# Attention units taken two at a time on TensorE, in a recurrence followed by a feed-forward layer

## The chip, the core and the metric

The kernel runs on one core of one Trainium2 chip. The metric is the device time of one execution in microseconds (us). A core has a matrix engine (TensorE, PE in the profile, with PEld for its weight loads), VectorE (DVE), ScalarE (ACT), GpSimd (POOL) and SyncE (SP), whose queue issues all DMAs of this kernel. Matrix products are written to PSUM, which has eight banks of 128 partitions by 512 fp32 columns.

## The reference, cut to what matters

```python
# 4 batches, 8 heads, 768 tokens, head_dim D=32, state N=16, chunk 32
log_a = np.log(np.clip(a, 1e-06, 1.0))
for c in range(S // 32):                       # chunks of 32 tokens
    cum = np.cumsum(la, axis=-1)               # la: log_a of this chunk
    L = np.exp(cum[:, :, :, None] - cum[:, :, None, :]) * causal
    M = np.einsum('bhin,bhjn->bhij', Cc, Bc) * L
    y_intra = np.einsum('bhij,bhjd->bhid', M, xc)
    y_inter = np.einsum('bhin,bhnd->bhid', Cc, state) * np.exp(cum)[..., None]
    y[:, :, sl] = y_intra + y_inter
    Bx = np.einsum('bhjn,bhjd->bhjnd', Bc, xc) * decay_from_j
    state = decay_full * state + np.sum(Bx, axis=2)
x = y as [3072 tokens, 256]
h = x @ w_in                                   # w_in 256 x 2048
g = np.maximum(h, 0) + np.log1p(np.exp(-np.abs(h)))
out = g @ w_out                                # w_out 2048 x 256
```

## The kernel before, in words

**Attention.** A unit is 128 tokens of one batch, all 8 heads; there are 24 units (4 batches of 6). For unit i, on TensorE: `score` makes two tiles sp (B by C products; for units 8 to 11 each is a 64-row product of 512 columns, L386; from unit 12 each is two full-array products of 256 columns, L391); `update` makes zp, the unit's contribution to the state (L416, four products on 32 of the array's columns, seen as 8 instructions); `read` multiplies the state before the unit with C into yp (L450, 32 rows by 64 columns of the array, 8 instructions; not for the first unit of a batch); `within` adds the products inside the unit to yp (L466, 32 columns of the array, 16 instructions). Around them VectorE and ScalarE make m from sp (`weigh`, L402), state and tb from zp, y from yp times the growth gg (`grow`, L477), and split y into a high and a low part xh, xl for the feed-forward layer (L480, L485). GpSimd makes the mask rm.

**Feed-forward.** Tokens go in six chunks of 512 (four units each). A step (j, k) is chunk j and 128 of the 2048 hidden columns: `first` makes hp with six products of 512 columns (L563); ScalarE applies softplus into e (L591) and copies it to gh (L597), VectorE makes gl = e - gh (L603); `second` adds six more products of 512 columns to two accumulators acc (L642). `second` of a step stands 8 steps behind its `first` (LAG). The buffers: e 3, gh 4, gl 4; six PSUM banks (`ps`) for hp, sp, zp, yp and others; two banks for acc.

**Order.** The first part, units 0 to 7 and 20 steps with the splitting of the weights, is a written list (ORDER), kept in that order on all engines; its instructions stand in the profile under L127, the line of the helper. From step 20 on nothing pins TensorE, VectorE, ScalarE or GpSimd: a scheduler with its own model of the times places each instruction, by order of the program where several are ready. DMAs on SP keep the order of the program everywhere. In the program, unit i has its place at step s = 20, 22, 25, 28 for units 8 to 11 and (i - 4)*4 after that: `prepare` and `attend_scores` at s, `attend_values` (spread, update, read, within, grow, rest) one or two steps later, and the loads of unit i + 2 at s + 1.

**Loads.** A unit's data is one tile un (3 buffers): x, B, C by token and by row (`U_S` columns) and, behind them, the rows for the scores. `split_unit` makes b_rows and c_rows from it for units from 12 on; c_rows has one buffer and is filled by two DMAs from c_all. The growth gg is loaded for three units at once.

Of the kernel before, what the change touches and what calls it, by code (L numbers as in the profile page):

```python
# [10 lines left out]
F32 = mybir.dt.float32  # L11
# [4 lines left out]
ALU = mybir.AluOpType  # L16
PSUM = bass.MemoryType.PSUM

P = 128
NB, NH, S, D, N = 4, 8, 768, 32, 16  # L20
# [51 lines left out]
LAG = 8  # L72
WRAW = 4
EARLY = 8
U_STEP = (20, 22, 25, 28)


def constants():
# [26 lines left out]
def recurrence_then_ffn(ctx: ExitStack, tc: tile.TileContext, fst, un, at, al, w_in, w_out, const, outT):  # L105
# [12 lines left out]
    class InOrder:  # L118
# [4 lines left out]

        def __getattr__(self, name):
            f = getattr(self.engine, name)
            if in_order[0]:
                return lambda *a, **k: tc.keep_in_program_order(f(*a, **k))  # L127
            return f

# [4 lines left out]
    def load(out, in_):  # L134

        tc.keep_in_program_order(nc.sync.dma_start(out, in_))  # L136
# [46 lines left out]
    def growth_on_chip(i, n):  # L183

        if i == 0:
            gg = p2.tile([P, 2, GU * P], F32, tag="gg", name="gg0")
            for v in range(GU):
                gg_s[v] = gg[:, :, v * P : v * P + P]
        gp = ps.tile([P, 512], F32, tag="ps", name=f"gp{i}")
        sums = kc[:, : NC * (P + SUB)].rearrange("p (c k) -> p c k", k=P + SUB)[:, :, :SUB]  # L190
        for v in range(n):
            for g in range(2):
                h0 = 2 * (i + v) + g
                PE.matmul(
                    gp[:, (2 * v + g) * P : (2 * v + g + 1) * P].rearrange("p (c k) -> p c k", k=SUB),
                    by_column[0][:, h0 * P : h0 * P + P],
                    sums,
                    start=True,
                    stop=True,
                )  # L200
        yield
        for v in range(n):
            A.activation(
                gg_s[i + v], gp[:, 2 * v * P : 2 * (v + 1) * P].rearrange("p (g t) -> p g t", g=2), AF.Exp, scale=-1.0
            )


    un_s, gg_s, st = {}, {}, {}

    def load_unit(i):  # L210
        if i < HEAD:
            un_s[i] = head_in["h"][:, i]
            load(un_s[i], fst[i, :, :U_S])
            return
        un_s[i] = p3.tile([P, U_END], F32, tag="un", name=f"un{i}")
        if i < FIRST:
            load(un_s[i][:, :F_END], fst[i])
        else:
            load(un_s[i], un[i - FIRST])


    def load_head_c(i):
# [1 line left out]

    def load_growth(i):
        b, u = divmod(i, NU)
        if u % GU == 0:
            gg = p2.tile([P, 2, GU * P], F32, tag="gg", name=f"gg{i}")
            for g in range(2):
                src = gd[b, g * 4 : g * 4 + 4, u * P : (u + GU) * P].unsqueeze(1).broadcast_to([4, D, GU * P])  # L230
                load(gg[:, g, :], src)
            for v in range(GU):
                gg_s[i + v] = gg[:, :, v * P : v * P + P]


    c_rows = cp.tile([P, NQ, 2, P], F32R, name="c_rows")

    def split_unit(i):
        if i < FIRST:
            return  # L240
        t = un_s[i]
        b_rows = p2.tile([P, NQ, P], F32R, tag="b_rows", name=f"b_rows{i}")

        def split(out, j):
            raw = t[:, U_S + j * NQ * P : U_S + (j + 1) * NQ * P].rearrange("p (q t) -> p q t", q=NQ)
            g, be = (kb[:, C_GB + v : C_GB + v + 1] for v in (2 * j, 2 * j + 1))
            A.activation(out, raw, AF.Copy, scale=be)
            V.scalar_tensor_tensor(out, raw, g, out.bitcast(F32), op0=ALU.mult, op1=ALU.add)

        c_all = p2.tile([P, NQ, P], F32R, tag="c_all", name=f"c_all{i}")  # L250
        split(c_all, 1)
        for e in range(2):
            rows = slice(64 * e, 64 * e + 64)
            load(c_rows[rows, :, e].bitcast(F32), c_all[rows].bitcast(F32))
        split(b_rows, 0)
        st[i] = b_rows
# [72 lines left out]
    def x_parts(t0):  # L329
        j = max(i for i in range(len(sizes)) if starts[i] <= t0)  # L330
        if j not in xparts:
            xparts[j] = [p3.tile([P, 2, 512], F32R, tag=f"x{v}", name=f"x{v}_{j}", bufs=3) for v in "hl"]
        return xparts[j], t0 - starts[j]
# [22 lines left out]
    def scale_b(i):  # L356
        b, u = divmod(i, NU)
        if u < NU - 1:
            bp = mid[i]["bp"] = p2.tile([P, NH, N], F32, tag="bp", name=f"bp{i}", bufs=3)
            V.tensor_tensor(  # L360
                bp,
                un_s[i][:, U_B:U_C].rearrange("p (h n) -> p h n", n=N),
                f_tok[b][0][:, u, :].unsqueeze(2).broadcast_to([P, NH, N]),
                op=ALU.mult,
            )
# [12 lines left out]
    def score(i, g):  # L378
        sp = mid[i]["sp", g] = ps.tile([P, 512], F32, tag="ps", name=f"sp{i}_{g}")
        if i < FIRST:  # L380
            rows = slice(64 * g, 64 * g + 64)
            if i < HEAD:
                t = head_in["l"][rows, i]
                PE.matmul(sp, t[:, :P], t[:, P:], start=True, stop=True)
                return
            PE.matmul(sp, un_s[i][rows, U_S : U_S + P], un_s[i][rows, U_S + P : F_END], start=True, stop=True)  # L386
            return
        b_rows = st[i]
        for v in range(2):
            q = 2 * g + v  # L390
            PE.matmul(  # L391
                sp[:, 2 * v * P : 2 * (v + 1) * P],
                b_rows[:, q],
                c_rows[:, q].rearrange("p e t -> p (e t)"),
                start=True,
                stop=True,
            )
# [11 lines left out]
    def update(i):  # L409

        b, u = divmod(i, NU)
        if u < NU - 1:
            bp = mid[i]["bp"]
            zp = ps.tile([P, 512], F32, tag="ps", name=f"zp{i}")
            for q in range(NQ):
                PE.matmul(  # L416
                    zp[32 * q : 32 * q + 32, : 2 * D],
                    bp[:, 2 * q : 2 * q + 2, :].rearrange("p h n -> p (h n)"),
                    un_s[i][:, U_X + 2 * q * D : U_X + 2 * (q + 1) * D],
                    start=True,  # L420
                    stop=True,
                )
            yield
            state[i] = p2.tile([P, 2 * D], F32, tag="state", name=f"state{i}", bufs=3)
            if u == 0:
                V.tensor_copy(state[i], zp[:, : 2 * D])
            else:
                V.scalar_tensor_tensor(
                    state[i], state[i - 1], f_row[b][:, u, NC : NC + 1], zp[:, : 2 * D], op0=ALU.mult, op1=ALU.add
                )  # L430

    def spread(i):

        if i % NU > 0:
            tb = mid[i]["tb"] = p2.tile([P, 2, D], F32, tag="tb", name=f"tb{i}", bufs=3)
            V.tensor_tensor(
                tb,
                state[i - 1].rearrange("p (e d) -> p e d", d=D),
                bd.unsqueeze(2).broadcast_to([P, 2, D]),
                op=ALU.mult,  # L440
            )
# [45 lines left out]
    def whole(steps):  # L487
        for _ in steps or ():
            pass

    def attend_scores(i):
        decays(i)
        for g in range(2):
            score(i, g)
            weigh(i, g)
        scale_b(i)
        scale_c(i)

    def attend_values(i):
        for f in (spread, update, read, within, grow, rest):  # L500
            whole(f(i))

# [168 lines left out]

    def prefetch(i):
        if i < NB * NU:
            load_unit(i)
            load_growth(i)

    def prepare(i):
        split_unit(i)  # L680
# [71 lines left out]
    def values(s):  # L752
        j, k = steps[s - LAG]
        if s - LAG >= DONE:
            second(j, k)
            if k == NFT - 1:
                finish(j)
            elif k == HALF - 1 and j < 2:
                keep_sums(j)
# [4 lines left out]
    def plan(s, f, *args):  # L764
        fills[s].append((f, args))

    for i in range(EARLY, NB * NU):
        s, wait = (U_STEP[i - EARLY], 1) if i - EARLY < len(U_STEP) else ((i - HEAD) * NFT // 4, 2)
        plan(s, prepare, i)
        plan(s, attend_scores, i)  # L770
        plan(s + wait, attend_values, i)
        if i + 2 < NB * NU:
            plan(s + 1, prefetch, i + 2)
    for i in range(EARLY, EARLY + 2):
        prefetch(i)
    for s in range(AHEAD, len(steps) + LAG):
        if s < len(steps):
            first(*steps[s])
            for _ in parts_of(*steps[s]):
                pass  # L780
        values(s)
        for f, args in fills[s]:
            f(*args)


# [48 lines left out]
```

## Time and profile before

| | |
|---|---|
| median of 3 runs | 341.94 us (340.47 to 342.95) |
| span of the profiled execution, first to last instruction | 338.8 us |
| PE busy | 328.7 us, 97% |
| DVE, ACT, POOL busy | 202.8, 171.7, 39.3 us |
| granted TensorE clock | 1.000 |

The page gives the span of the profiled execution, 338.8 us, and no other time for it; the runs' median is 3.1 us above the span. In the profile's rows, a group is named by its line, engine and operation, then what it writes and reads. In the timeline, the columns are the start in us, the us from the start of a piece to its end, and the piece; the ends of matrix products are modelled and neighbours overlap, so what a product costs is read from one start to the next.

### The profile page before, as it was taken

Reading aid. Unit: us, or ns where it says so; the run is one execution under the profiler, and the core shown is the slowest. Engines: PE = TensorE matmul, PEld = TensorE weight load, DVE = VectorE, ACT = ScalarE, POOL = GpSimd, SP = SyncE. Lnnn points to the kernel's source line nnn. Section 1 sums busy time; section 2 is a strip of 40 time slices with the busy share of each in tenths; the row PEclk is TensorE's granted clock in tenths of the full one; section 3 lists DMA queues with packets and bytes.
Section 4 is the critical chain, followed back from the end, with each engine's and each line's share of the span. In section 5 each row is a group of like instructions: output and inputs, shape, how many; then the busy total and the mean of one; then the engine's idle time right before and its main releaser. Section 6 shows DMA issues by size and latency. Waiting matters only on the chain.

```text
span 338.8 us, 5271 instructions
## 1 busy us (share of the span) xinstructions
PE 328.7 (97%) x2047; PEld 249.4 (74%) x2047; DVE 202.8 (60%) x394; ACT 171.7 (51%) x319; POOL 39.3 (12%) x32
## 2 busy tenths in 40 slices
PE   8789998999999999999999999999999999999995
PEld 4446657887666678778778778778778778888885
DVE  0899989996946444864765464777474342232242
ACT  4845666875715435445445455445445244444450
POOL 2434510000111010110112010111010000000000
PEclk9999999999999999999999999999999999999999
DMA  7964533573032205416434205443203100010001
GB/s 233 396 228 138 220 106 104 188 259 120 3 98 114 93 0 189 133 39 186 126 61 141 95 0 188 122 106 99 94 2 93 33 0 0 2 55 8 2 0 62
DMA packets 19376, 35.01 MB, mean 103 GB/s; under 512 B 1432, under 2 KB 10136, under 8 KB 19352
## 3 DMA queue, kind: packets, MB, share of 16 engines
q1 hardware_dynamic: 19352, 34.68, 31.5%
q8 instruction: 16, 0.26, 0.3%
q14 instruction: 8, 0.07, 0.1%
HBM read 28.28 MB, written 3.24 MB: 93 GB/s over the span
## 4 chain that ended last, share of the span: by engine, by line
PE 86%; DVE 6%; DMA 5%; SPq 1%; issue 1%; ACT 0%
PE hp L563 32%; PE acc L642 32%; PE hp L127 6%; PE acc L127 6%; PE yp L466 3%; DMA gg<-gd 3%; DMA head_in_l<-in_fst 2%; PE yp L450 2%; PE sp L391 2%; DVE m L127 1%; DVE w L127 1%; PE sp L386 1%; SPq L136 1%; PE zp L416 1%; PE end L127 1%
## 5 line engine op out<-in xcount | busy, mean ns | idle before, releaser
L603 DVE TENSOR_TENSOR gl<-e,gh 128x512 fp32r<-128x512 f32 x76 | 55.7, 734 | 61.3 <-ACT gh L597 61.1
L597 ACT CAST gh<-e 128x512 fp32r<-128x512 f32 x76 | 47.1, 620 | 61.1 <-PE acc L642 60.3
L591 ACT ACTIVATE e<-hp 128x512 f32<-128x512 f32 x76 | 45.1, 596 | 42.4 <-DVE gl L603 38.5
L563 PE MATMUL hp<-xh,wih 128*128 128x512 f32 x152 | 61.3, 405 | 0.0
L642 PE MATMUL acc<-gl,woh 128*128 128x512 f32 x155 | 60.6, 391 | 0.0
L642 PE MATMUL acc<-gh,wol 128*128 128x512 f32 x155 | 60.5, 391 | 0.0
L642 PE MATMUL acc<-gh,woh 128*128 128x512 f32 x155 | 59.6, 391 | 0.0
L563 PE MATMUL hp<-xl,wih 128*128 128x512 f32 x152 | 59.5, 392 | 0.0
L563 PE MATMUL hp<-xh,wil 128*128 128x512 f32 x152 | 59.3, 391 | 0.0
L345 POOL TENSOR_SCALAR_AFFINE_SELECT rm<-fc 128x1024 f32<-128x1024 f32 x16 | 23.8, 1487 | 187.7 <-DVE m L402 167.8
L563 PEld LDWEIGHTS hp<-xh,wih 128*128 128x128 f32 x152 | 28.5, 188 | 10.7 <-issue 3.1
L642 PEld LDWEIGHTS acc<-gh,woh 128*128 128x128 f32 x155 | 29.1, 188 | 6.8 <-issue 0.8
L642 PEld LDWEIGHTS acc<-gh,wol 128*128 128x128 f32 x155 | 29.1, 188 | 6.2
L642 PEld LDWEIGHTS acc<-gl,woh 128*128 128x128 f32 x155 | 29.1, 188 | 6.1 <-issue 0.2
L563 PEld LDWEIGHTS hp<-xh,wil 128*128 128x128 f32 x152 | 28.5, 188 | 6.3
L563 PEld LDWEIGHTS hp<-xl,wih 128*128 128x128 f32 x152 | 28.6, 188 | 5.1
L402 DVE TENSOR_TENSOR m<-sp,rm 128x512 f32<-128x512 f32 x32 | 20.9, 685 | 7.9 <-PE sp L391 6.3
L127 DVE SCALAR_TENSOR_TENSOR w<-wraw,w 128x512 int32<-128x512 int32 x32 | 23.1, 729 | 0.2
L127 PE MATMUL hp<-xh,wih 128*128 128x512 f32 (+1 forms) x48 | 17.7, 368 | 2.0 <-DVE m L127 1.4
L127 PE MATMUL hp<-xl,wih 128*128 128x512 f32 (+1 forms) x48 | 17.0, 354 | 0.0
L127 PE MATMUL hp<-xh,wil 128*128 128x512 f32 (+1 forms) x48 | 17.0, 354 | 0.0
L127 POOL TENSOR_SCALAR_AFFINE_SELECT rm<-fc 128x1024 f32<-128x1024 f32 x8 | 14.0, 1764 | 20.8 <-DVE m L127 15.0
(109 smaller groups left out, 409.6 us busy)
## 6 DMA issues: line engine op xcount, KB each, us to landing
un<-in_un SPq DMA_DIRECT2D x12, 768.0 KB, 4.4
un<-in_fst SPq DMA_DIRECT2D x8, 576.0 KB, 6.1
wraw<-in_w_in SPq DMA_DIRECT2D x8, 512.0 KB, 3.4
wraw<-in_w_out SPq DMA_DIRECT2D x8, 512.0 KB, 5.2
c_rows<-c_all SPq DMA_DIRECT2D x24, 128.0 KB, 2.4
out_t<-o SPq DMA_DIRECT2D x11, 256.0 KB
gg<-gd SPq DMA_DIRECT2D x14, 192.0 KB
head_in_l<-in_fst SPq DMA_DIRECT2D x4, 320.0 KB, 6.2
```

Of the source, the lines that this page charges most:

```text
L127: return lambda *a, **k: tc.keep_in_program_order(f(*a, **k))
L136: tc.keep_in_program_order(nc.sync.dma_start(out, in_))
L345: Pl.affine_select(out=rm.rearrange("p h c i -> p (h c) i"), in_=fc[:, u].rearrange("p h c -> p (h c)").unsqueeze(2).broadcast_to([P, NH * ...
L391: PE.matmul(sp[:, 2 * v * P : 2 * (v + 1) * P], b_rows[:, q], c_rows[:, q].rearrange("p e t -> p (e t)"), start=True, stop=True,)
L402: V.tensor_tensor(mid[i]["m"][:, 4 * g : 4 * g + 4].rearrange("p h t -> p (h t)"), mid[i].pop(("sp", g)), mid[i]["rm"][:, 4 * g : 4 * g + ...
L450: PE.matmul(yp[q // 2][out], tb[rows].rearrange("p e d -> p (e d)"), cc[rows].rearrange("p c i -> p (c i)"), start=True, stop=False,)
L466: PE.matmul(yp[g][32 * hh : 32 * hh + 32], un_s[i][:, U_X + h * D : U_X + (h + 1) * D], m[:, h, :], start=u == 0, stop=True,)
L563: PE.matmul(h[:, c0:c1], w[:, c, fs], x[:, c, c0:c1], start=i == 0, stop=i == 5)
L591: A.activation(e, h, AF.Softplus)
L597: A.copy(gh, e)
L603: V.tensor_tensor(gl, e, gh.bitcast(F32), op=ALU.subtract)
L642: PE.matmul(acc[:, c0:c1], wo[v, k // HK][:, k % HK, es], g[:, c0:c1], start=start and i == 0, stop=stop and i == 2,)
```

## The change

From unit 8 on the units go in pairs, i and i + 1, every eight steps. All TensorE instructions, of the loop too, now keep the order of the program. `values_pair` issues, one behind the other: the reads of both units, the products within both, and the state products zp of the next pair; the two units share the two banks of yp (columns 0 to 127 and 128 to 255), the two state products share one bank. The state products of units 8 and 9 stand alone ahead of the loop. y, xh and xl are made for both units in one instruction each (y in two). The scores of a pair stand two steps apart (s + 2 and s + 4), the joint visit at s + 6; s is 18, 24 and then (i - 4)*4.

The unit's tile is divided in two, un (`U_S` columns, 6 buffers) and ub (the rows for the scores, 2 buffers), each with a load of its own; un is requested further ahead. From unit 6 on the growth is loaded for two units at once, with 3 buffers. The scratch memory for DMAs issued by GpSimd is set to 2048 bytes.

```diff
-U_STEP = (20, 22, 25, 28)
+PAIR_STEP = {8: 18, 10: 24}
...
-            if in_order[0]:
+            if in_order[0] or self.engine is nc.tensor:
                 return lambda *a, **k: tc.keep_in_program_order(f(*a, **k))
...
-        un_s[i] = p3.tile([P, U_END], F32, tag="un", name=f"un{i}")
-        if i < FIRST:
-            load(un_s[i][:, :F_END], fst[i])
-        else:
-            load(un_s[i], un[i - FIRST])
+        load_values(i)
+        load_rows(i)
+
+    def load_values(i):
+        un_s[i] = p3.tile([P, U_S], F32, tag="un", name=f"un{i}", bufs=6)
+        load(un_s[i], fst[i, :, :U_S] if i < FIRST else un[i - FIRST, :, :U_S])
+
+    def load_rows(i):
+        ub_s[i] = p3.tile([P, U_END - U_S], F32, tag="ub", name=f"ub{i}", bufs=2)
...
-            for v in range(GU):
+        n = GU if i < NU else 2
...
+    def read_pair(i):
+        yp = mid[i]["yp"] = [ps.tile([P, 512], F32, tag="ps", name=f"yp{i}_{g}")[:, : 2 * P] for g in range(2)]
+        begun = set()
+        for v in range(2):
+            if (i + v) % NU > 0:
+                tb, cc = mid[i + v]["tb"], mid[i + v]["cc"]
+                for q in range(NQ):
+                    rows, out = slice(32 * q, 32 * q + 32), slice(64 * (q % 2), 64 * (q % 2) + 64)
+                    PE.matmul(
+                        yp[q // 2][out, v * P : v * P + P],
+                        tb[rows].rearrange("p e d -> p (e d)"),
+                        cc[rows].rearrange("p c i -> p (c i)"),
+                        start=q not in begun,
+                        stop=False,
+                        skip_group_check=True,
+                    )
+                    begun.add(q)
+
+    def within_pair(i):
+        for v in range(2):
+            for g in range(2):
+                for hh in range(4):
+                    h = g * 4 + hh
+                    PE.matmul(
+                        yp[g][32 * hh : 32 * hh + 32, v * P : v * P + P],
+                        un_s[i + v][:, U_X + h * D : U_X + (h + 1) * D],
+                        m[:, h, :],
+                        start=False,
+                        stop=True,
+                        skip_group_check=True,
+                    )
+
+    def grow_pair(i):
+        y = p2.tile([P, 2, 2 * P], F32, tag="yy", name=f"yy{i}")
+        for g in range(2):
+            V.tensor_tensor(y[:, g], mid[i]["yp"][g], gg_s[i, 2][:, g], op=ALU.mult)
...
+        A.copy(hi, y)
+        V.tensor_tensor(xl[:, :, c0 : c0 + 2 * P], y, hi.bitcast(F32), op=ALU.subtract)
+
+    def values_pair(i):
+        for v in range(2):
+            spread(i + v)
+        read_pair(i)
+        within_pair(i)
+        update_pair(i + 2)
+        grow_pair(i)
+
+    def update_pair(i):
+        some = [v for v in range(2) if i + v < NB * NU and (i + v) % NU < NU - 1]
...
-    for i in range(EARLY, NB * NU):
-        s, wait = (U_STEP[i - EARLY], 1) if i - EARLY < len(U_STEP) else ((i - HEAD) * NFT // 4, 2)
-        plan(s, prepare, i)
-        plan(s, attend_scores, i)
-        plan(s + wait, attend_values, i)
-        if i + 2 < NB * NU:
-            plan(s + 1, prefetch, i + 2)
+    for i in range(EARLY, NB * NU, 2):
+        s = PAIR_STEP.get(i, (i - HEAD) * NFT // 4)
+        for v in range(2):
+            plan(s + 2 * v, prepare, i + v)
+            plan(s + 2 * v + 2, attend_scores, i + v)
+            if i + 2 + v < NB * NU:
+                plan(s + 4, scale_b, i + 2 + v)
+                plan(s + 2 * v + 3, prefetch, i + 2 + v)
+            if i + 4 + v < NB * NU:
+                plan(s + 7, prefetch_values, i + 4 + v)
+        plan(s + 6, values_pair, i)
...
+    update_pair(EARLY)
...
-    nc = _bacc.Bacc("TRN2", target_bir_lowering=False, num_devices=1)
+    nc = _bacc.Bacc("TRN2", target_bir_lowering=False, num_devices=1, dynamic_dma_scratch_size=2048)
```

More of the change, by code (lines that the diff above doesn't have):

```diff
@@ L185, in growth_on_chip @@
         if i == 0:
-            gg = p2.tile([P, 2, GU * P], F32, tag="gg", name="gg0")
+            gg = p3.tile([P, 2, GU * P], F32, tag="gg", name="gg0")
             for v in range(GU):
@@ L205, in growth_on_chip @@
             )
-    un_s, gg_s, st = {}, {}, {}
+    un_s, ub_s, gg_s, st = {}, {}, {}, {}
     def load_unit(i):
@@ L214, in load_unit @@
             return
-        un_s[i] = p3.tile([P, U_END], F32, tag="un", name=f"un{i}")
+        load_values(i)
[5 more added lines that the diff above has]
+        ub_s[i] = p3.tile([P, U_END - U_S], F32, tag="ub", name=f"ub{i}", bufs=2)
         if i < FIRST:
-            load(un_s[i][:, :F_END], fst[i])
+            load(ub_s[i][:, : F_END - U_S], fst[i, :, U_S:])
         else:
-            load(un_s[i], un[i - FIRST])
+            load(ub_s[i], un[i - FIRST, :, U_S:])
     def load_head_c(i):
@@ L226, in load_growth @@
         b, u = divmod(i, NU)
-        if u % GU == 0:
-            gg = p2.tile([P, 2, GU * P], F32, tag="gg", name=f"gg{i}")
+        n = GU if i < NU else 2
+        if u % n == 0:
+            gg = p3.tile([P, 2, GU * P], F32, tag="gg", name=f"gg{i}")[:, :, : n * P]
             for g in range(2):
-                src = gd[b, g * 4 : g * 4 + 4, u * P : (u + GU) * P].unsqueeze(1).broadcast_to([4, D, GU * P])
+                src = gd[b, g * 4 : g * 4 + 4, u * P : (u + n) * P].unsqueeze(1).broadcast_to([4, D, n * P])
                 load(gg[:, g, :], src)
-            for v in range(GU):
+            for v in range(n):
                 gg_s[i + v] = gg[:, :, v * P : v * P + P]
+            if n == 2:
+                gg_s[i, 2] = gg
     c_rows = cp.tile([P, NQ, 2, P], F32R, name="c_rows")
@@ L240, in split_unit @@
             return
-        t = un_s[i]
+        t = ub_s[i]
         b_rows = p2.tile([P, NQ, P], F32R, tag="b_rows", name=f"b_rows{i}")
         def split(out, j):
-            raw = t[:, U_S + j * NQ * P : U_S + (j + 1) * NQ * P].rearrange("p (q t) -> p q t", q=NQ)
+            raw = t[:, j * NQ * P : (j + 1) * NQ * P].rearrange("p (q t) -> p q t", q=NQ)
             g, be = (kb[:, C_GB + v : C_GB + v + 1] for v in (2 * j, 2 * j + 1))
@@ L385, in score @@
                 return
-            PE.matmul(sp, un_s[i][rows, U_S : U_S + P], un_s[i][rows, U_S + P : F_END], start=True, stop=True)
+            PE.matmul(sp, ub_s[i][rows, :P], ub_s[i][rows, P : F_END - U_S], start=True, stop=True)
             return
@@ L423, in update, with advance @@
             yield
-            state[i] = p2.tile([P, 2 * D], F32, tag="state", name=f"state{i}", bufs=3)
-            if u == 0:
-                V.tensor_copy(state[i], zp[:, : 2 * D])
-            else:
-                V.scalar_tensor_tensor(
-                    state[i], state[i - 1], f_row[b][:, u, NC : NC + 1], zp[:, : 2 * D], op0=ALU.mult, op1=ALU.add
-                )
+            advance(i, zp[:, : 2 * D])
+    def advance(i, zp):
+        b, u = divmod(i, NU)
+        state[i] = p2.tile([P, 2 * D], F32, tag="state", name=f"state{i}", bufs=4)
+        if u == 0:
+            V.tensor_copy(state[i], zp)
+        else:
+            V.scalar_tensor_tensor(state[i], state[i - 1], f_row[b][:, u, NC : NC + 1], zp, op0=ALU.mult, op1=ALU.add)
     def spread(i):
@@ new lines, in within_pair @@
+    def within_pair(i):
+        yp = mid[i]["yp"]
+        for v in range(2):
+            m = mid[i + v]["m"]
+            for g in range(2):
[9 more added lines that the diff above has]
+                    )
@@ new lines, in grow_pair @@
+    def grow_pair(i):
+        y = p2.tile([P, 2, 2 * P], F32, tag="yy", name=f"yy{i}")
+        for g in range(2):
+            V.tensor_tensor(y[:, g], mid[i]["yp"][g], gg_s[i, 2][:, g], op=ALU.mult)
+        (xh, xl), c0 = x_parts(i * P)
+        hi = xh[:, :, c0 : c0 + 2 * P]
+        A.copy(hi, y)
[7 more added lines that the diff above has]
+        grow_pair(i)
@@ new lines, in update_pair @@
+    def update_pair(i):
+        some = [v for v in range(2) if i + v < NB * NU and (i + v) % NU < NU - 1]
+        if some:
+            zp = ps.tile([P, 512], F32, tag="ps", name=f"zp{i}")
+        for v in some:
+            for q in range(NQ):
+                PE.matmul(
+                    zp[32 * q : 32 * q + 32, 2 * D * v : 2 * D * v + 2 * D],
+                    mid[i + v]["bp"][:, 2 * q : 2 * q + 2, :].rearrange("p h n -> p (h n)"),
+                    un_s[i + v][:, U_X + 2 * q * D : U_X + 2 * (q + 1) * D],
+                    start=v == 0,
+                    stop=True,
+                    skip_group_check=True,
+                )
+        for v in some:
+            advance(i + v, zp[:, 2 * D * v : 2 * D * v + 2 * D])
@@ L495, in attend_scores @@
             weigh(i, g)
-        scale_b(i)
         scale_c(i)
-    def attend_values(i):
-        for f in (spread, update, read, within, grow, rest):
-            whole(f(i))
     raws = {}
@@ L675, in prefetch, with prefetch_values @@
         if i < NB * NU:
-            load_unit(i)
+            load_rows(i)
             load_growth(i)
+    def prefetch_values(i):
+        if i < NB * NU:
+            load_values(i)
     def prepare(i):
@@ L765, in plan @@
         fills[s].append((f, args))
-    for i in range(EARLY, NB * NU):
-        s, wait = (U_STEP[i - EARLY], 1) if i - EARLY < len(U_STEP) else ((i - HEAD) * NFT // 4, 2)
-        plan(s, prepare, i)
-        plan(s, attend_scores, i)
-        plan(s + wait, attend_values, i)
-        if i + 2 < NB * NU:
-            plan(s + 1, prefetch, i + 2)
[L774 to L777, printed above, removed]
+    for i in range(EARLY, NB * NU, 2):
[9 more added lines that the diff above has]
+        plan(s + 6, values_pair, i)
+    for i in range(EARLY, EARLY + 4):
+        prefetch_values(i)
+        if i < EARLY + 2:
+            prefetch(i)
+            scale_b(i)
+    update_pair(EARLY)
+    for s in range(min(AHEAD, min(fills)), len(steps) + LAG):
+        if AHEAD <= s < len(steps):
             first(*steps[s])
@@ L780, in recurrence_then_ffn @@
                 pass
-        values(s)
-        for f, args in fills[s]:
+        if s >= AHEAD:
+            values(s)
+        for f, args in sorted(fills[s], key=lambda v: v[0] is prepare):
             f(*args)
```

## The prediction

> **What bounds the kernel now.** I began with the page: which engine is busy, and at what clock.
>
> ```profile
> PE 328.7 (97%) x2047; PEld 249.4 (74%) x2047; DVE 202.8 (60%) x394; ACT 171.7 (51%) x319; POOL 39.3 (12%) x32
> ```
>
> A busy PE may still hide gaps, so next the waits of PE, and one window from the loop's first product to the end.
>
> ```profile
> PE hp L127 <- DVE m L127: 1.4, 1, 1.4
> ...
> 86.35:332.13 245.78, 245.78 (x1466) 1.00 0.23 72
> ```
>
> The longest wait of PE, shown here, and all others carry L127, the ordered first part. From 86.35 to 332.13 us it is busy for the whole 245.78 at clock 1.00: the loop is bound by what TensorE issues, so I split that time by products. The same window, grouped by form:
>
> ```profile
> L563 PE MATMUL hp<-xh,wih 128*128 128x512 f32 x152 | 61.3, 405 | 0.0
> L642 PE MATMUL acc<-gl,woh 128*128 128x512 f32 x155 | 60.6, 391 | 0.0
> ...
> L466 PE MATMUL yp<-m,un 128*32 128x128 f32 x256 | 10.7, 279 | 0.0
> L391 PE MATMUL sp<-c_rows,b_rows 128*128 128x256 f32 x48 | 7.9, 281 | 0.0
> L450 PE MATMUL yp<-cc,tb 32*64 32x128 f32 x112 | 7.1, 293 | 0.0
> L386 PE MATMUL sp<-un 64*128 64x512 f32 x16 | 4.5, 641 | 0.0
> L416 PE MATMUL zp<-un,bp 128*32 128x64 f32 x104 | 4.1, 231 | 0.0
> ```
>
> hp and acc have three such rows each, so 3x152 + 3x155, and 8 under L127: 929 products of 512 columns. Means overlap, so prices come from starts, in the timeline:
>
> ```profile
> 86.90 1.13 PE L386 MATMUL sp<-un 64*128 64x512 f32 x4
> ...
> 128.40 0.39 PE L642 MATMUL acc<-gh,woh 128*128 128x512 f32 x1
> ...
> 133.84 0.64 PE L391 MATMUL sp<-c_rows,b_rows 128*128 128x256 f32 x4
> 134.31 0.40 PE L563 MATMUL hp<-xh,wih 128*128 128x512 f32 x1
> ...
> 148.10 0.39 PE L642 MATMUL acc<-gh,wol 128*128 128x512 f32 x1
> 148.42 0.32 PE L416 MATMUL zp<-un,bp 128*32 128x64 f32 x8
> 148.67 0.45 PE L450 MATMUL yp<-cc,tb 32*64 32x128 f32 x8
> 149.04 0.64 PE L466 MATMUL yp<-m,un 128*32 128x128 f32 x16
> 149.62 0.50 PE L563 MATMUL hp<-xh,wih 128*128 128x512 f32 x1
> 149.96 0.40 PE L563 MATMUL hp<-xl,wih 128*128 128x512 f32 x1
> 150.20 0.40 PE L563 MATMUL hp<-xh,wil 128*128 128x512 f32 x1
> ```
>
> From 128.40 to 133.84 stand 24 acc products: 0.2267 us each. Four sp take 0.47. Now a **visit** to the small products: the step into them is 0.32 instead of 0.23 (+0.09); the first full product behind them holds the next one back to 0.34 (+0.11), and the few after it start some 0.01 late each (+0.04 together): 0.24 per visit, whatever is inside. The bodies are zp 0.25, read 0.375, within 0.575.
>
> Check: 929 x 0.2267 = 210.6; 12 sp groups x 0.47 = 5.7; the four scores of units 8 to 11, 1.06 each (86.90 to the next start at 87.96), 4.2. That leaves 25.3. Bodies: 13 x 0.25 + 14 x 0.375 + 16 x 0.575 = 17.7, and about 1.0 more because the scheduler broke the reads of units 10 and 11 in two. Visits, counted down the timeline from the one at 86.90 to the last, which ends in the within at 277.02: 26 (zp often stands apart from yp), x 0.24 = 6.2. Sum 24.9: the loop's time is explained to 0.4 us without any stall. So the change can win only bodies and visits, 25 us in all, and can lose by stalls that are absent today.
>
> **The change, part by part.** *Visits.* In fixed order there are 8 joint visits, one for the state products of units 8 and 9, and the 4 scores of units 8 to 11: 13 instead of 26, **-3.1 us**.
>
> *Bodies.* What does a second unit cost in the same mode? The first part has one group of 16 zp:
>
> ```profile
> 12.84 0.43 PE L127 MATMUL zp<-head_in_h,bp 128*32 128x64 f32 x16
> ...
> L416 PEld LDWEIGHTS zp<-un,bp 128*32 128x32 f32 x104 | 2.0, 108 | 4.6 <-issue 3.9 <-ACT e L591 0.7
> ```
>
> 16 take 0.43 where 8 take 0.32: the second eight add 0.11 instead of 0.25. A within has twice the instructions, each of twice the columns: I take 4 x 0.11 = 0.44. A second read has the eight instructions at twice the columns: between 0.22 and the full 0.375, I take 0.24, nearer the zp row. zp behind within stays in 32-column form: 0.11 a unit. Sums: reads, 6 pairs with both and 2 with one (units 12 and 18 have none): 6 x 0.615 + 2 x 0.375 = 4.4; within 8 x (0.575 + 0.44) = 8.1; zp 11 x 0.11 + (0.25 + 0.11) = 1.6. That is 14.1 against 18.7: **-4.6 us**. If joining gave nothing but the unbroken reads, -1.0.
>
> [...]
>
> *Sharing banks.* Two units' outputs lie in one bank of yp, at other columns. Already today two of the four products of a read go to one bank together, in the body of 0.375; the second unit's follow behind the first's, so no more meet in a bank at once. I price the sharing at 0, at most 6 x 0.135 = 0.8, the other end of the read.
>
> *Fixed order.* The scheduler could fill a late operand with 24 acc products (128.40); now whatever is late stops all of PE. Three places. First, **the chunk's edge**: pairs 10, 14, 18 and 22 visit at steps 30, 46, 62, 78, and the chunk's first hp is two steps later. Cover, from the end of the within piece: 12 x 0.2267 and the way out, 2.8 us (0.1 to 0.2 more where zp follows). The chain behind it, at the last unit:
>
> ```profile
> 277.02 0.64 PE L466 MATMUL yp<-m,un 128*32 128x128 f32 x16
> ...
> 278.01 0.48 DVE L477 TENSOR_TENSOR y<-yp,gg 128x128 f32<-128x128 f32 x2
> 279.05 0.43 DVE L485 TENSOR_TENSOR xl<-y,xh 128x256 fp32r<-128x256 f32 x1 [0.56 <-ACT xh L480]
> ...
> 278.62 0.40 ACT L480 CAST xh<-y 128x256 fp32r<-128x256 f32 x1
> ...
> L127 DVE TENSOR_TENSOR o_end<-end,o_end 128x256 f32<-128x256 f32 x2 | 0.8, 425 | 1.8 <-PE end L127 1.8
> ...
> L603 DVE TENSOR_TENSOR gl<-e,gh 128x512 fp32r<-128x512 f32 x76 | 55.7, 734 | 61.3 <-ACT gh L597 61.1
> L597 ACT CAST gh<-e 128x512 fp32r<-128x512 f32 x76 | 47.1, 620 | 61.1 <-PE acc L642 60.3
> L591 ACT ACTIVATE e<-hp 128x512 f32<-128x512 f32 x76 | 45.1, 596 | 42.4 <-DVE gl L603 38.5
> ```
>
> y starts 0.35 after the piece's end (278.01 against 277.66), xh 0.13 after y, xl 0.03 after xh. With joint sizes: 0.35, two y of 256 columns out of PSUM (0.425 each, the o_end row), 0.13, xh of 512 columns (0.62 like gh), 0.03, xl (0.73 like gl). xh is there after 1.95 and wanted after 2.8, xl after 2.7 and wanted after 3.0. It fits by 0.3 to 0.85; one DVE instruction of 0.7 in front of y breaks it. Second, **the ring**: gh(n) waits for acc of n-4, gl for gh, softplus of n+3 for gl: 0.62 + 0.73 + 0.60, with hand-overs 2.1 us, against a step of 12 x 0.2267 = 2.72 before the next hp wants a bank when a visit holds three of the six. Third, **the start**: acc of the last ordered step waits for gl.
>
> ```profile
> 83.71 0.29 DVE L360 TENSOR_TENSOR bp<-un,ft 128x128 f32<-128x128 f32 x1 [2.26 <-DMA un<-in_fst]
> ...
> 86.12 0.68 DVE L127 TENSOR_TENSOR gl<-e,gh 128x512 fp32r<-128x512 f32 x1
> ...
> 86.35 0.39 PE L563 MATMUL hp<-xh,wih 128*128 128x512 f32 x1
> ```
>
> In fixed order PE, which today goes on with the loop's first hp at 86.35, would stand until that gl ends at 86.80: 0.45. DVE was late there because bp had held it 2.26 us for a unit's load, which is now asked for earlier: between 0 and 0.45. I charge 0.6 for the three together.
>
> *Loads and the rest.* There are 26 more DMA issues (20 units twice, gg 20 instead of 14), on a queue that mostly waits for others. One lies on the path:
>
> ```profile
> DVE y L127 <- DMA gg<-gd: 1.4, 1, 1.4
> ...
> 35.48 0.42 SPq L136 DMA_DIRECT2D un<-in_fst  x1
> 35.95 1.12 SPq L136 DMA_DIRECT2D gg<-gd  x2
> ...
> c_rows<-c_all SPq DMA_DIRECT2D x24, 128.0 KB, 2.4
> ...
> 134.51 1.27 SPq L136 DMA_DIRECT2D c_rows<-c_all  x2
> ```
>
> The gg of units 6 and 7 is asked for right behind un7, which becomes two issues (+0.4), but it carries two thirds of the bytes, and the wait behind it is 1.4 in all: between +0.4 and -1.4, I take 0. c_rows of a pair's second unit must wait for the first unit's score: issues 1.27 and landing 2.4, 3.7 of two steps' 5.4. y, xh and xl in fewer instructions and the moved scalings are DVE and ACT work beside PE (60% and 51% busy). The scratch size concerns DMAs issued by GpSimd; all issues here are SP's.
>
> **Sum.** 338.8 - 3.1 - 4.6 + 0.6 = 331.7 us of span; with the 3.1 between span and median: **334.8 us**.
>
> **Rivals.** *Edges late* (chance 0.15): DVE has a gl or a weigh (0.7 each) ahead of y at the four edges, 0.7 to 1.3 each, 3 to 5 us: 337 to 340. For it: the margin at xl is 0.3. Against it: DVE is 60% busy, and at steps 30, 46, 62 and 78 no weigh is due. *No discount for joined bodies* (0.08): only visits and unbroken reads, -4.1 + 0.6: 338.4. The zp row speaks against it. [...] *Head of the line, slower* (0.11): VectorE's order is fixed by the scheduler's model, and it already stands in front of PE:
>
> ```profile
> DVE state L428 <- PE zp L416: 13.3, 9, 2.4
> ```
>
> If such a wait lies ahead of a gl, softplus is late, no bank comes free, and PE stands. It decides once the wait passes the ring's 0.6 us; at 2.4, twice a pair (state, weigh), it costs up to 1.8 x 2 x 8 = 28; at half of them 14, and 334.2 + 14 = 348. Against it: DVE's biggest wait is for gh (61.1 us), so gl usually has room. *It does not do what it says* (0.03): PE keeps visits apart, nothing won, 342. The forecast (331.5 to 337) has 0.60; the remaining 0.03 is a first part that runs late by 3 us or more, 338 to 341.
>
> The range is 331.5 (all of the gain, gg6 sooner, the runs' low end 1.5 under the median) to 340.0. Within 1% of 341.94, about what a measurement can tell from no change, is 338.5 to 345.4. Faster: 0.60, the 0.08, half of the edges: 0.74. Slower 0.11. Same 0.15.
>
> **What would show it.** Right: from the loop's start PE busy without waits, 13 visits, zp directly behind within with about 0.11 per unit, joint bodies near 1.85 us, and hp and acc alternating by six. Wrong: PE waits for xh or xl at the four edges, for gl at the start, or hp held up for a bank with DVE waiting for zp or sp; bodies of 2.4 would show that joining saves nothing.

## The result and the profile after

The changed kernel took 340.9 us (median of 20 runs, 337.86 to 344.24), the kernel before 342.07 beside it (20 runs): a ratio of 0.994, 95% interval 0.9913 to 0.9966. Forecast was 334.8, and 340.0 was the range's upper end. In a second comparison the same file gave 1.002 (0.9989 to 1.005). Medians are of all runs, ratios of the fast ones alone. The two intervals don't meet, so a difference of half a per cent says little here. The change is no faster by anything worth having: some 6 of the 7 us that were forecast are missing.

The page of the changed kernel, its waits of PE, and the window that answers to the loop's before:

```profile
span 339.0 us, 5271 instructions
...
PE 323.7 (95%) x2047; PEld 251.3 (74%) x2047; DVE 188.9 (56%) x370; ACT 170.9 (50%) x311; POOL 40.6 (12%) x32
...
PEclk9999999999999999999979999999999999999999
```

```profile
PE hp L127 <- ACT e L668: 5.3, 5, 1.9
...
PE acc L127 <- DVE gl L127: 1.0, 1, 1.0
...
PE sp L127 <- DMA c_rows<-c_all: 0.4, 1, 0.4
```

```profile
87.59:332.51 244.92, 239.13 (x1451) 191.75 (x1446) 113.78 (x213) 114.10 (x193) 21.25 (x14) 0.99 0.26 73
```

PE is busy for 5 us less than before, in a span of the same length: the work did shrink, and waits came in its place. Before, the loop had none. To put them in one sum I use one stretch that all kernels have: from the last state product of the ordered part to the first product of the `end` group. Timeline of PE, before, then after:

```profile
77.56 0.32 PE L127 MATMUL zp<-un,bp 128*32 128x64 f32 x8
...
332.13 0.28 PE L127 MATMUL end<-gh,woh 128*128 128x256 f32 x1
```

```profile
75.60 0.32 PE L127 MATMUL zp<-un,bp 128*32 128x64 f32 x8
...
87.23 0.43 PE L127 MATMUL zp<-un,bp 128*32 128x64 f32 x16
...
119.44 0.67 PE L127 MATMUL yp<-cc,tb 32*64 32x128 f32 x16
120.03 1.08 PE L127 MATMUL yp<-m,un 128*32 128x128 f32 x32
120.93 0.41 PE L127 MATMUL zp<-un,bp 128*32 128x64 f32 x16
121.27 0.50 PE L127 MATMUL hp<-xh,wih 128*128 128x512 f32 x1
...
332.51 0.28 PE L127 MATMUL end<-gh,woh 128*128 128x256 f32 x1
```

The stretch is 254.57 before and 256.91 after. The forecast of visits and bodies (-3.1 - 4.6) makes it 246.9 without any stall, so 10.0 us have to be found. Most of them lie behind the joint visits, and one visit shows how:

```profile
169.83 0.67 PE L127 MATMUL yp<-cc,tb 32*64 32x128 f32 x16
170.43 1.08 PE L127 MATMUL yp<-m,un 128*32 128x128 f32 x32
171.41 0.32 PE L127 MATMUL zp<-un,bp 128*32 128x64 f32 x8
173.67 0.50 PE L127 MATMUL hp<-xh,wih 128*128 128x512 f32 x1 [1.95 <-ACT e L668]
...
174.83 0.63 PE L127 MATMUL hp<-xl,wih 128*128 128x512 f32 x1
...
177.82 0.46 PE L127 MATMUL acc<-gh,wol 128*128 128x512 f32 x1
```

First, hp has no free bank until a softplus (ACT e) ends: 2.26 us from the start of zp to hp where another visit takes 0.23 to 0.34. Then, from 174.83 to 177.82, seven products take 0.427 each in place of 0.2267. Why was softplus late? ScalarE, then VectorE, then the DMA queue, in the same stretch:

```profile
169.54 0.72 ACT L258 ACTIVATE c_all<-ub,kb 128x512 fp32r<-128x512 f32 x1 [3.33 <-DMA ub<-in_un]
...
170.78 0.58 ACT L668 ACTIVATE e<-hp 128x512 f32<-128x512 f32 x1
...
173.02 0.60 ACT L668 ACTIVATE e<-hp 128x512 f32<-128x512 f32 x1 [1.16 <-DVE gl L680]
```

```profile
170.57 0.29 DVE L371 TENSOR_TENSOR bp<-un,ft 128x128 f32<-128x128 f32 x1 [2.72 <-DMA un<-in_un]
...
172.31 0.68 DVE L680 TENSOR_TENSOR gl<-e,gh 128x512 fp32r<-128x512 f32 x1
```

```profile
159.90 0.57 SPq L136 DMA_DIRECT2D ub<-in_un  x1
160.52 1.17 SPq L136 DMA_DIRECT2D gg<-gd  x2
161.79 0.41 SPq L136 DMA_DIRECT2D ub<-in_un  x1
162.24 0.91 SPq L136 DMA_DIRECT2D un<-in_un  x2
165.46 1.34 SPq L136 DMA_DIRECT2D c_rows<-c_all  x2
```

ScalarE stands 3.33 us in front of a c_all for the second unit's rows, with the softplus at 170.78 behind it; VectorE stands 2.72 us in front of a bp for un, with gl behind it. The rows and values they wait for were issued at 161.79 and 162.24, right behind the growth gg; they arrive 7.7 and 8.3 us later. The chain of waits goes through the first load of rows, issued ahead of gg, and through the c_rows behind it, whose end VectorE's next write of c_all waits for, at 170.78, also ahead of gl:

```profile
159.90 3.88 DMA ub<-in_un
...
166.16 4.58 DMA c_rows<-c_all
```

A load takes 3.9 us ahead of gg and 7.7 to 8.3 behind it, and c_rows takes 4.58 instead of the 2.4 that the prediction showed. Over the run, the waits of ScalarE, before and then after:

```profile
ACT c_all L247 <- DMA un<-in_un: 11.9, 11, 2.4
```

```profile
ACT c_all L258 <- DMA ub<-in_un: 25.1, 11, 3.3
```

### The profile page after: what moved, and what is told of

The parts are those of the page before. It is cut to its first block, busy times and chain, and to the rows that moved or that the text cites. A ratio compares the mean times of both kernels' runs of the same rounds, so it can differ in the third digit from the quotient of the medians.

```text
span 339.0 us, 5271 instructions
## 1 busy us (share of the span) xinstructions
PE 323.7 (95%) x2047; PEld 251.3 (74%) x2047; DVE 188.9 (56%) x370; ACT 170.9 (50%) x311; POOL 40.6 (12%) x32
## 4 chain that ended last, share of the span: by engine, by line
PE 64%; DMA 15%; DVE 8%; SPq 4%; ACT 4%; issue 3%; ACTq 0%; DVEq 0%
PE hp L127 28%; PE acc L127 28%; DMA ub<-in_un 7%; SPq L136 4%; DMA c_rows<-c_all 4%; PE sp L127 3%; PE yp L127 2%; DMA un<-in_fst 2%; DMA head_in_l<-in_fst 2%; DVE w L127 2%; ACT e L668 1%; DVE m L127 1%; ACT c_all L258 1%; DVE gl L680 1%; PE end L127 1%
## 5 line engine op out<-in xcount | busy, mean ns | idle before, releaser
L127 PE MATMUL hp<-xh,wih 128*128 128x512 f32 (+1 forms) x200 | 78.6, 393 | 7.3 <-ACT e L668 5.3
L127 PE MATMUL hp<-xl,wih 128*128 128x512 f32 (+1 forms) x200 | 76.7, 383 | 0.0
L127 PE MATMUL hp<-xh,wil 128*128 128x512 f32 (+1 forms) x200 | 76.5, 382 | 0.0
L127 PE MATMUL acc<-gl,woh 128*128 128x512 f32 x188 | 73.9, 393 | 1.0 <-DVE gl L127 1.0
L127 PE MATMUL acc<-gh,woh 128*128 128x512 f32 x188 | 74.2, 395 | 0.0
L668 ACT ACTIVATE e<-hp 128x512 f32<-128x512 f32 x76 | 45.3, 596 | 56.9 <-DVE gl L680 54.5
L127 PE MATMUL acc<-gh,wol 128*128 128x512 f32 x188 | 73.5, 391 | 0.0
L127 PEld LDWEIGHTS hp<-xh,wih 128*128 128x128 f32 x200 | 37.7, 188 | 19.6 <-ACT e L668 6.2
L127 PEld LDWEIGHTS hp<-xh,wil 128*128 128x128 f32 x200 | 37.7, 189 | 7.5
L127 PEld LDWEIGHTS hp<-xl,wih 128*128 128x128 f32 x200 | 37.7, 189 | 6.7 <-DVE xl L546 0.5
L127 PEld LDWEIGHTS acc<-gl,woh 128*128 128x128 f32 x188 | 35.6, 189 | 9.3 <-DVE gl L127 1.9
L127 PEld LDWEIGHTS acc<-gh,woh 128*128 128x128 f32 x188 | 35.6, 189 | 8.0 <-issue 0.2
L127 PEld LDWEIGHTS acc<-gh,wol 128*128 128x128 f32 x188 | 35.6, 189 | 7.5
L127 DVE SCALAR_TENSOR_TENSOR w<-wraw,w 128x512 int32<-128x512 int32 x32 | 23.1, 728 | 0.1
L127 POOL TENSOR_SCALAR_AFFINE_SELECT rm<-fc 128x1024 f32<-128x1024 f32 x8 | 14.0, 1766 | 20.7 <-DVE m L127 14.9
L127 ACT ACTIVATE e<-hp 128x512 f32<-128x512 f32 x20 | 11.9, 597 | 9.1 <-DVE gl L127 6.9
```

The lines of the kernel that those rows point to most:

```text
L668: A.activation(e, h, AF.Softplus)
```

## The experiments

**The same file again**, to see what repeats.

> The changed kernel once more, timed beside the others on one chip. Both theories: 0.994 of before, near 341 us, TensorE with about 5 us of waits for softplus (hp for e) and 1 us for gl. It gives the number that the other runs are held against.

342.6 against 341.07, a ratio of 1.002 (0.9989 to 1.005). The waits of hp for softplus are there again ("PE hp L127 <- ACT e L668: 5.8, 5, 2.4"), and the half-speed stretch is too, at another place (last section).

**The growth last.** gg goes behind the other loads of the pair (at the start behind un11).

```diff
+
+    def prefetch_growth(i):
+        if i < NB * NU:
             load_growth(i)
...
+        plan(s + 7, prefetch_growth, i + 2)
...
+    prefetch_growth(EARLY)
```

> The changed kernel with the growth loads moved: the gg of the next pair is asked for after all other loads of its round (behind the un of the pair after) instead of between the first and the second unit's rows; at the start behind un11 instead of ahead of un9. Theory A (the slow gg transfers hold up what is queued behind them; ScalarE's c_all and VectorE's bp stand at the head of their queues waiting for it, so softplus and gl come late and TensorE stands): un9 lands about 4 to 5 us after its issue instead of 7.3, the 1.2 us wait at the start goes, the second unit's rows land 4 to 5 us after their issue instead of 7.7, hp's waits for e fall from 5.3 to under 2 us; 336 us, 0.983 of before. Theory B (the ring of six banks, of which a joint visit holds three, is too short by itself): the start wins 1.2 us, hp's waits for e stay near 5 us; 339.5 us, 0.992.

341.83, 1.0019 (0.9993 to 1.0045): no gain, and both theories missed the time. But the waits moved. Those of PE:

```profile
PE sp L127 <- DMA c_rows<-c_all: 6.7, 4, 3.1
...
PE hp L127 <- ACT e L668: 0.4, 1, 0.4
```

The wait at the start is gone and hp's fell from 5.3 to 0.4, which bears theory A out in part: the waits were those of gg. But something else now stands behind it. The DMA queue:

```profile
152.31 1.02 SPq L136 DMA_DIRECT2D out_t<-o  x2
...
154.37 1.19 SPq L136 DMA_DIRECT2D gg<-gd  x2
155.66 7.94 SPq L136 DMA_DIRECT2D c_rows<-c_all  x4
```

The store of the outputs, which waits for VectorE's o, heads the queue; everything then goes out at once, and c_rows, issued directly behind gg, lands 5.10 later by the chain of waits. So it isn't the rows or the values as such: what stands behind gg is late. One half-speed stretch is here as well, behind the longest of these waits.

**The rows earlier as well**: the second edit on top of the first, ub two steps sooner.

```diff
-                plan(s + 2 * v + 3, prefetch, i + 2 + v)
+                plan(s + 2 * v + 1, prefetch, i + 2 + v)
```

> As the run before it, and the rows (ub) of the next pair's units asked for two steps earlier, the first ahead of the c_rows copy that waits for this pair's first score. Theory A: ScalarE no longer waits long for ub (25 us in the changed kernel, under 8 here), hp's waits for e are gone or under 0.5 us; 334.5 us, 0.978 of before. Theory B: as in the run before, 339.5 us.

347.7 (342.93 to 350.93), 1.0141 (1.0094 to 1.0188): slower, and far from the 334.5 of theory A. gg is still right ahead of a c_rows in the queue, and PE waits for that; one of four such rows:

```profile
136.24 1.19 PE L127 MATMUL sp<-c_rows,b_rows 128*128 128x256 f32 x4 [3.87 <-DMA c_rows<-c_all]
```

ScalarE waits for ub as long as in the changed kernel (26.0 us, where under 8 was expected). An earlier request for the rows doesn't help while gg stands between the loads. Against the run before, PE waits 8.9 us for c_rows in place of 6.7, and four windows at half clock lie in the loop in place of one (last section). That points to where the time went, but the profile is of a run that took 348.43, so the sizes aren't those of a typical run.

**The order of TensorE left free**, all else as in the changed kernel.

```diff
-            if in_order[0] or self.engine is nc.tensor:
+            if in_order[0]:
```

> The changed kernel with TensorE's order in the loop left to the scheduler again (one condition taken back), pairs, banks and loads as changed. Theory A: the late loads stay, but the scheduler has moved acc products in front, or not, by its model alone; TensorE's waits fall under 3 us if it did, visits are more than 13; 338 to 341 us. Theory B: with free order no bank is missed, waits near 0; 336 us.

339.19, 0.9933 (0.9902 to 0.9964), 3.4 us under the changed kernel in the same comparison (342.6). That is within theory A's 338 to 341. The scheduler hides hp's waits and leaves 2.8 us in front of within, for m, and 1.2 at the start; it does not bring the gain back.

**Loads in the gap.** The values at s + 5, the growth at s + 6, where nothing that is soon needed follows (the c_rows issued next, at 164.02, is used at 181.82); the rows stay where the change has them.

```diff
+
+    def prefetch_growth(i):
+        if i < NB * NU:
             load_growth(i)
...
-                plan(s + 7, prefetch_values, i + 4 + v)
+                plan(s + 5, prefetch_values, i + 4 + v)
+        plan(s + 6, prefetch_growth, i + 2)
...
+    prefetch_growth(EARLY)
```

> The changed kernel with the loads in another order: per pair the rows of the next two units, then the un of the two after them (two steps earlier than in the changed kernel), and the growth last, at step s + 6, where nothing that is soon needed follows. Theory A, narrowed by the runs so far (the slow gg transfers hold whatever is queued behind them: the rows in the changed kernel, the c_rows copy of a pair's first unit when gg stands last at s + 7): neither waits now; TensorE's waits in the loop under 1.5 us, no window at half clock in the loop, 333 us, 0.976 of before. Theory C (the queue's own order, stores that wait at its head and copies that wait for a score, delays loads with or without gg): waits of 4 us or more stay, 338 us or more.

334.44 (332.64 to 336.06), 0.976 (0.972 to 0.9801). The only wait of PE in the loop, and the stretch:

```profile
PE hp L127 <- DVE xl L546: 0.2, 1, 0.2
```

```profile
76.48 0.32 PE L127 MATMUL zp<-un,bp 128*32 128x64 f32 x8
...
86.48 0.43 PE L127 MATMUL zp<-un,bp 128*32 128x64 f32 x16
...
324.36 0.28 PE L127 MATMUL end<-gh,woh 128*128 128x256 f32 x1
```

247.88: the forecast's 246.9 and 1.0. Nothing of the products, the pairs, the banks or the order was touched.

**No growth loads.** From unit 10 on no gg is loaded; the growth of units 8 and 9 stands in for the others, so these outputs are other numbers.

```diff
+        if i > EARLY:
+            for v in range(n):
+                gg_s[i + v] = gg_s[EARLY + (i + v) % 2]
+            gg_s[i, 2] = gg_s[EARLY, 2]
+            return
```

> The changed kernel without the growth loads from unit 10 on: all later pairs take the growth of units 8 and 9 (this part of the result is left out). Everything else, the order of the other loads too, is as changed. Theory A: hp's waits for e (5 us) and the windows at half clock go, the wait of 1.2 us at the start stays (gg of unit 8 is still ahead of un9): 334 us, 0.979. Theory C: waits of 4 us or more stay, 338 us or more.

335.37, 0.9784 (0.9738 to 0.9831). hp's waits for softplus fall from 5.3 to 0.2, and no window at half clock lies in the loop; the 1.0 us at the start stays, as it must, because gg of units 8 and 9 is still ahead of un9. The DMAs, with the median time to landing in the last column:

```profile
ub<-in_un SPq DMA_DIRECT2D x12, 512.0 KB, 3.8
...
c_rows<-c_all SPq DMA_DIRECT2D x24, 128.0 KB, 2.4
```

**The kernel before, with TensorE's order fixed**, and nothing else of the change.

```diff
-            if in_order[0]:
+            if in_order[0] or self.engine is nc.tensor:
```

> The kernel before with one condition added: TensorE keeps the order of the program in the loop; units stay single, loads and banks as before. Both theories: 20 visits instead of 26 (-1.4 us) and no broken reads (-1.0). Theory A: one load per unit, ahead of its gg, lands in 4.4 us, so few waits are added: 339 to 341 us, 0.995. If fixed order is itself what costs (a rival to both), waits of 4 us or more appear: 344 us.

351.97, 1.0273 (1.0232 to 1.0314), far above what any theory gave. PE waits 8.2 us for c_rows ("PE sp L127 <- DMA c_rows<-c_all: 8.2, 4, 2.2"), which the free order had covered with other products. Here gg is not the cause: in the chain of waits, c_rows takes its usual 2.44 or 2.45 us all four times. It is issued late, because out_t, the store of a chunk's outputs, stands ahead of it in the queue and waits for o, which needs the chunk's last acc. So theory C, which the two runs above speak against for the changed kernel, describes this one. With two windows at half clock (from 133.27 and 215.19, 1.6 each by the last section), the sum is 8.2 + 3.2 - 2.4 (the expected gain) = 9.0; the medians differ by 9.25. The fixed order makes every late load a stall. In the paired kernel it costs nothing by itself, as the next run shows.

**Loads in the gap, the order free.** Both edits shown above.

> As the run with the growth at s + 6, and TensorE's order in the loop left to the scheduler. Theory A: nothing is left to fill, so as that run within 1 us: 333 us, 0.976. If fixed order is itself what costs: 2 us or more below that run.

334.28, 0.975 (0.9706 to 0.9794), not to be told from the fixed order's 334.44. With the loads in time, fixing the order neither costs nor gains.

**Why is gg so slow?** Two theories were left: its place and its many small pieces, or its shape. The trace records each piece that the DMA engines move, and the size tells the load: 1 KB is gg, 4 KB rows, 2 KB values, 512 B c_rows. A window of the kernel with loads in the gap in which only pieces of gg start; the last two columns are the DMA share and GB/s:

```profile
167.50:168.00 0.50, 0.50 (x4) 0.42 (x3) 0.50 (x2) 0.06 (x1) 0.06 (x1) 1.00 0.27 90
```

A share of 0.27 is some 4 of 16 DMA engines (0.27 x 16 = 4.3). The source is 4 heads by 32 copies by the tokens, with the heads as the slowest dimension. That these two fours belong together is a guess of mine: the traces have no engine for a piece. The next run tests it.

The pieces also show how gg holds what stands behind it. With the growth last, 384 of the 512 pieces of c_rows have started by 158.41; then none starts until 159.83, when gg starts its last (159.87); the other 128, a quarter, follow by 160.70. With the loads in the gap the same 384 and 128 stand on both sides of 166.78 to 168.42, and gg ends at 168.92. Without growth loads the 512 start within 1.45 us without a gap. So a quarter of the load behind (128 of 512 pieces) starts only when gg is about done; that these are the pieces of the engines which gg keeps is my reading of this quarter and of the 0.27. In the changed kernel gg ends at 166.7, and what is left drains in the end at the same share of 0.27, values and the last quarter of c_rows (384 of its 512 pieces have started by 170.01, the other 128 start from 170.50 to 171.49):

```profile
170.00:171.50 1.50, 1.50 (x54) 1.16 (x52) 0.93 (x3) 1.50 (x4) 0.00 (x0) 1.00 0.27 75
```

So I cut the load otherwise, in the place that the change gave it: one head of each half per load, 32 copies outermost.

```diff
-            for g in range(2):
-                src = gd[b, g * 4 : g * 4 + 4, u * P : (u + n) * P].unsqueeze(1).broadcast_to([4, D, n * P])
-                load(gg[:, g, :], src)
+            for hh in range(4):
+                src = gd[b, hh::4, u * P : (u + n) * P].unsqueeze(0).broadcast_to([D, 2, n * P])
+                load(gg[32 * hh : 32 * hh + 32], src)
```

> The changed kernel; only the growth load is cut otherwise: four loads of 32 partitions (one head of each half per load) in place of two of 128, in the same place of the queue. In the kernel with the growth in the gap, the half microseconds in which nothing but a growth load is under way show a DMA share of 0.27 to 0.28, about 4 of 16 engines: the source's slowest dimension was the 4 heads, now it is 32 copies. Theory A1 (the growth load is slow because few DMA engines carry it, and holds what is queued behind it): it now lands in some 3 us instead of 8, the rows' second load and the values no longer wait, the waits of hp for softplus fall from 5.3 to under 1 us, and the time comes near that of the kernel with the growth in the gap: 334 to 336. Theory A2 (its place in the queue or its many small pieces are what hold the rest, not how many engines carry it): as the changed kernel, 340 to 343, or a little slower for two more issues of about 0.45 us. Theory B (six banks are too few) has fallen already and expects 341.

336.51, 0.9833 (0.9779 to 0.9887), for an edit of three lines that adds two issues per pair. The waits and the DMA row:

```profile
PE hp L127 <- ACT e L668: 3.1, 5, 1.0
```

```profile
gg<-gd SPq DMA_DIRECT2D x36, 64.0 KB, 4.0
```

gg lands in 4.0 us, the wait at the start is gone, and this profile has no half-speed stretch in the loop. The time is 0.5 us above what A1 gave, and hp still waits 3.1 us where A1 said under 1. So the shape alone brings most of the gain, with gg in its old place; what is left of hp's waits needs the other place as well (0.5 in the next run). A2, which expected 340 to 343, has fallen.

**Both**, loads in the gap and the growth cut in four.

> Both at once: the growth in the gap, and cut in four loads of 32 partitions. Theory A1: little is left to win, since PE has 0.2 us of waits in the loop there; 333.5 to 335, not to be told from 334.4. Theory A2: the same, or up to 1 us slower for the two more issues a pair ahead of c_rows.

333.86 (332.37 to 335.17), 0.9749 (0.9696 to 0.9802): as expected, nothing to be told from 334.44. Loads that are in time gain nothing by being faster. This is the version to keep.

**The kernel before, its growth cut in four** (the same edit with its three units).

> The kernel before, with the growth load cut in four loads of 32 partitions (192 KB in all as before in each half). No wait of PE in its loop is for a load, and the one wait for the growth is VectorE's 1.4 us in the first part. Theory A1: the loop as before, the first part up to 1.4 us sooner; 340.5 to 342, within 1% of no change. If the free order had hidden late loads at a price, it would be 338 or less.

339.36, 0.9919 (0.9894 to 0.9945), some 1 us under what was expected. Timeline of PE:

```profile
76.02 0.32 PE L127 MATMUL zp<-un,bp 128*32 128x64 f32 x8
...
330.57 0.28 PE L127 MATMUL end<-gh,woh 128*128 128x256 f32 x1
```

The stretch is 254.55, the 254.57 of before: its loop had hidden the slow load at no price. The first part ends 1.54 sooner, about the 1.4 us that VectorE had waited for gg; the profiles' spans differ by 1.7 (337.1 against 338.8). The ratio makes it 2.8; where the rest comes from isn't shown.

## Why the prediction was wrong, step by step

**Visits and bodies: right.** hp and acc alternate by six, in thirteen visits. The joint visit at 119.44 reads 0.59 for the read (predicted 0.615), 0.90 for within (1.015); the zp of two units take 0.34 behind it, those of one, at other visits, 0.23: 0.11 for the second, as taken. The kernel with loads in the gap shows the whole -7.7 but for 1.0. The rival "no discount" falls: the second eight zp cost 0.11 here, where a zp body by itself was 0.25 in the kernel before.

**Sharing banks, the chunk's edge: right.** In the changed kernel nothing waits for xh or xl at steps 30, 46, 62 or 78; with the loads in the gap one hp waits 0.2 us for xl, where the margin was put at 0.3. "Edges late" didn't happen.

**The first part: 0 was taken with a bound of -1.4;** it came 1.96 sooner in this profile (75.60 against 77.56), and VectorE's wait for gg is gone from it. The profiles of kernels with the change's first part lie between 75.08 and 77.71, so the size isn't settled by one.

**Fixed order, "I charge 0.6 for the three together": this step failed.** The chunk's edge held, the start and the ring did not, because what feeds them came late. The start cost 1.6 (from 75.60 to 87.23 are 11.63, against 10.00 in the kernel with loads in the gap), because VectorE's bp waited for un9 behind gg:

```profile
78.52 0.29 DVE L371 TENSOR_TENSOR bp<-un,ft 128x128 f32<-128x128 f32 x1 [2.81 <-DMA un<-in_fst]
```

The prediction had read the same wait in the trace of before (2.26) and assumed that the earlier request would shorten it. The ring cost 5.3 by PE's waits for softplus, one c_rows 0.4, and the half-speed stretch behind one of these waits 1.6. Together 8.9 of the 10.0; the remaining 1.1 is about what the kernel without these stalls has too. The ring's own sum was right: with the loads in time hp doesn't wait for softplus.

Under it lies a term that was put at nothing, in the sentence "26 more DMA issues ... on a queue that mostly waits for others". Issues were counted, and landings were taken one by one from the trace of before: 2.4 for c_rows. A queue was seen as instructions on SP, not as transfers behind a slow one. The queue of before, which I didn't look at for this:

```profile
139.70 0.34 SPq L136 DMA_DIRECT2D un<-in_un  x1
140.09 1.16 SPq L136 DMA_DIRECT2D gg<-gd  x2
152.74 1.03 SPq L136 DMA_DIRECT2D out_t<-o  x2
```

A unit's load stood ahead of gg, and the next request came 12 us later; the change put gg between the rows of a pair, with the values right behind. The diff showed that order, and the 1.4 us wait for gg, which the prediction quoted, was a hint that this load was slow.

**The rival "head of the line" had the right shape:** an engine stands in front of gl or softplus, no bank comes free, PE stands. It named the wrong wait (VectorE for PE's zp; it was ScalarE and VectorE for DMAs) and too large a price (14), and had a chance of 0.11. (The parts given for "faster" add to 0.755, not 0.74; nothing hangs on it.)

## What to carry to other kernels

A fixed order on the bound engine is as good as the arrival of the loads: with them in time it cost nothing in the paired kernel (334.44 against 334.28), with c_rows late it cost the kernel before 2.7% (351.97 against 342.72). When a change moves loads, write out the queue in its new order and ask for each transfer what stands ahead of it and how long that takes to land, not how long its issue takes. And when a broadcast load is small but slow, look at the DMA share while it runs alone: here it was 0.27, about what a quarter of the engines would make. Three lines mended that here (gg then landed in 4.0 us, and the ratio to the kernel before was 0.9833). What it cost here was not its own time, but the part of the loads behind it that it kept waiting, 128 of 512 pieces of c_rows.

## What the hardware showed that was not expected

Behind some waits (1.95 us in the changed kernel, 3.06 in the one with the growth last) TensorE ran at half clock for one window of 3.41 us. The windows of the changed kernel and of the same file run again, with the clock in the third column from the right:

```profile
174.53:177.95 3.42, 3.42 (x10) 2.64 (x9) 2.29 (x7) 1.22 (x2) 0.00 (x0) 0.50 0.00 0
```

```profile
229.41:232.82 3.41, 3.41 (x10) 2.65 (x9) 2.34 (x8) 1.22 (x2) 0.00 (x0) 0.50 0.02 5
```

Each costs 1.6 (seven products at 0.427 in place of 0.2267, and the two at its edges), which nearly doubles the price of the stall ahead of it.

Whether it comes seems to depend on where the wait falls. In one trace the starts of these windows lie whole multiples of 3.413 us apart (133.27 and 215.19 in the kernel before with fixed order are 24 of them; 174.53 and 338.37 in the changed kernel, the second at the end of its span, are 48), so I count the borders of all windows from one: an estimate where the clock stayed full. In the changed kernel the wait of 1.95 lies inside the window ahead of 174.53, and half clock followed. In the same file run again, the longest wait, 2.36 up to 175.34, crosses a border at 174.80 and had no such effect; two shorter ones up to 226.70 and 228.56 (0.76 and 1.43) share the window ahead of 229.41 but for 0.06, and had it. So in these traces the length of a wait alone doesn't decide; by this count, how much of it lies in one window bears on it too. A limit isn't shown: 1.67 inside one window did nothing in the changed kernel and 1.91 nothing in the kernel before with fixed order (the wait up to 270.00), but 1.71 was enough in the run with TensorE's order free.

In the changed kernel PE was idle for 1.95 us of the 3.41 ahead of 174.53, so a window that is idle only in part was enough there. The profiles of the kernels with loads in the gap and of the kernel before show no such window in their loops.
